# Two-scale attention with a gated convolution on one core: another model in the scheduler, another order of the first transfers, weights converted with more work on ScalarE

## The chip, the cores and the metric

The kernel runs on one core of a Trainium2 chip. The metric is the device time of one execution in microseconds (us). Before the change it is 425.0 us, the median of three runs (424.87 to 425.13).

The engines are named as the profile names them: PE (TensorE, with PEld for its weight loads), DVE (VectorE), ACT (ScalarE), POOL (GpSimd) and SP (SyncE, which here only issues transfers). Each engine executes its own list of instructions in the order in which it was written. An instruction whose input is not there holds up everything behind it on that engine.

## The reference, cut to what matters

```python
q_d, k_d, v_d = mean over 4 neighbouring positions          # B, H, S, D = 8, 8, 576, 64
out_up  = repeat(softmax(q_d @ k_d.T / 8) @ v_d, 4)          # coarse attention, 144 x 144
scores  = where(|i - j| < 4, q @ k.T / 8, -1e9)              # local attention, a band
x       = out_up + softmax(scores) @ v                       # to (8, 576, 512)
gate    = sigmoid(sum over 5 taps of conv_w[t] * x shifted)  # causal, for each channel
out     = (gate * (x @ w_val)) @ w_out                       # w_val, w_out: 512 x 512
```

q, k and v are 32-bit floats. w_val, w_out and conv_w are handed to the kernel as 64-bit floats, and their bits are turned into 32-bit values on the chip.

## The kernel before, in words

**Pairs and blocks.** The attention is cut into 32 pairs p: batch p // 4 and two of its eight heads, whose 2 x 64 channels fill 128 partitions. For the projections x is one long row of 8 x 576 = 4608 columns, cut into eight blocks j of 504 columns and two of 288. Block 0 can be projected when the four pairs of batch 0 are done.

**One pair**, by the names in the profile. Local attention: `sl` (scores on PE), `mx` and `sub` (DVE), the exponential (ACT), `sm` (row sums, DVE, with a small add behind it at L533), `rs` (reciprocal), `pexp` (the two halves of the normalised band, on DVE or POOL), `tl` (two transposes on PE, named tl0 and tl1), `pt` (their copy to SBUF, ACT), `x` (the product with v, PE). Coarse attention: `half` and `qs` (sums of four positions of q and k), `sd` (scores), `cmx` and `cbi` (DVE), `pd` (exponential on ACT; its normalising on DVE, POOL or ACT), `tc` (two transposes), `pdt` (their copy, ACT), `odp` (the product with the coarse v, PE), `od` (its copy, ACT). `xt` on DVE adds the two results. Then `xhs` (rounded part, ACT) and `xls` (remainder) feed the projection; five `gp` steps (the first on ACT, four on DVE) and a tanh on ACT make the gate.

**Products.** A projection is done as three products, high by high, low by high and high by low. A piece of `val` (block j, output chunk c) is three matmuls of 504 columns; `h` = gate * val, which is split into `hh` (ACT) and `hl` (DVE or POOL) and goes through three matmuls for `out`, whose copy `ob` is written to memory.

**Coarse sums.** For batch 0 the sums of four are made on the chip: `half`/`qs` for q and k, `vhalf` (L475) and `vd` (L479) for v, from the loaded `qk` and `vg`. From batch 1 on the transfers make them: one transfer from SP writes the first of four positions, and three more from POOL (L405) add the others to it in memory-to-SBUF accumulation.

**Weights.** w_val and w_out come in 16 chunks of 128 x 256 64-bit numbers (`raw_v`, `raw_o`, L860). For each, ACT takes out two fields (L824 `cv_l`, L826 `cv_a`), DVE makes three passes (L829 shift, L834 sign, L840 add of the low bits), ACT casts to `wh` (L872), and DVE or POOL makes the remainder `wl` (L875). Two raw buffers are there.

**What sets the order.** A list scheduler in the kernel file (`Planner`) is given each operation's engine, a duration in ns, what it depends on and which buffers it needs free. It simulates the engines once, at build time, and the program is written out in that order; where `either` gives two engines, the simulation also picks. Before the change TensorE's order is a fixed list (`tensor_order`, from the strings below); only the other four engines are ordered by due times, some of which are set or shifted by hand in `BIAS`, `FIRST`, `LATE` and `DUE`. A P in the strings is a piece of a projection, a quote mark is the pair before.

```python
START = "sl tl0' tl1' sd tc1' tc0' odp' x'"
START3 = "tl1' sd sl tl0' tc0' tc1' x' odp'"
START4 = "sl tc0' tl1' P tl0' sd tc1' odp' x' P P P"
STEADY = "P P sl tc1' tc0' sd tl1' tl0' P P P P P P odp' x'"
```

Warm-up matmuls (L378, on a constant) are put where the simulation sees TensorE idle.

Of the kernel before, what the change touches and what calls it, by code (L numbers as in the profile page):

```python
# [12 lines left out]
U16 = mybir.dt.uint16  # L13
I64 = mybir.dt.int64
# [5 lines left out]
NC = 4  # L20
P = 128
# [51 lines left out]
def last_reader(b):  # L73
# [7 lines left out]
SB, TB, VB = 3, 2, 3  # L81

# [19 lines left out]
BIAS = {  # L102
    "pdt1": -8000, "h2.0": 2000, "hlo3.0": -1000, "norm1": 2000, "fld": 4000, "h2.1": -8000, "h3.0": -4000,
    "cwfld": 2000, "xl": -8000, "pvb": 2000, "od": -1000, "xt0": -2000, "exp": 1000, "rcp": -2000,
    "cexp0": -1000, "h1.1": 4000, "cmx0": -1000, "hhi3.0": -2000,
}
FIRST = {("qk", 0): -2e6, ("qk2", 0): -1.9e6}
DUE = {("raw", 0): -799008, ("vw", 0): -799729, ("raw", 2): 10251, ("qk", 1): -799570}
# [5 lines left out]

class Planner:
# [25 lines left out]

    def tensor_order(self, order, bufs):
        ops = self.ops
        prev, users = None, {t: [] for t in bufs}
# [12 lines left out]
    def lat(self, o):
        return o["late"] or (self.LOAD if "SP" in o["opts"] else self.LAT)

    def switch(self, a, b):  # L160
# [4 lines left out]
        pairs = {("x", "odp"), ("odp", "x"), ("x", "x"), ("x", "tl"), ("odp", "tl"), ("x", "tc"), ("odp", "tc")}
        return 40 if (a, b) == ("sl", "sd") else 33 if (a, b) in pairs else 3

    def rank(self):
        ops = self.ops
        for o in ops.values():  # L170
            o["in"] = [k for k in o["deps"] + o["free"] if k in ops]
            o["succ"] = []
        for k, o in ops.items():
# [17 lines left out]
        for k, due in ((k, due) for k, due in {**DUE, **FIRST}.items() if k in ops):  # L191
            ops[k]["due"] = due

    def simulate(self):
# [5 lines left out]
        free, queue, events, start, end, who = {}, {}, [], {}, {}, {}  # L200
        for o in ops.values():
            for e in o["opts"]:
                free[e] = self.BEGIN.get(e, 0)
                queue.setdefault(e, [])
        for e, t in free.items():
            events.append((t, e, ()))
        heapq.heapify(events)

        def ready(k):
            for e in ops[k]["opts"]:  # L210
# [915 lines left out]
```

## Time and the profile before

| | |
|---|---|
| median of the runs | 425.0 us |
| span of the profiled execution | 420.9 us |
| PE busy | 382.3 us, 91% |
| DVE busy | 332.8 us, 79% |
| ACT busy | 248.1 us, 59% |
| POOL busy | 122.4 us, 29% |
| moved by DMA | 70.28 MB, mean 167 GB/s |

The execution that was profiled has a span of 420.9 us, from its first to its last instruction; the median of the runs is 4.1 us longer, which is what lies around the span. The busy shares are means over the whole span, and the head of the kernel (loading, converting weights, the first pairs) differs from the steady part.

### The profile page before, as it was taken

The numbers are of one execution on the slowest core, as the hardware profiler recorded it, in microseconds if no ns is written. First come the engines' busy times: TensorE is split into PE (matmuls) and PEld (weight loads), VectorE is DVE, ScalarE is ACT, GpSimd is POOL, SyncE is SP. The second block draws the span as 40 slices with busy tenths as digits, with TensorE's granted clock in tenths as the row PEclk, the third lists the DMA queues.
The fourth block names the chain that finished last, engine by engine and source line by source line (L and its number), as shares of the span: only waits on it lengthen the run. The fifth ranks groups of instructions, "written<-read, shape, count | busy, mean of one in ns | idle before, by whom it ended". The sixth has DMA issues, their size and how long they took to land.

```text
span 420.9 us, 13961 instructions
## 1 busy us (share of the span) xinstructions
PE 382.3 (91%) x5889; PEld 299.6 (71%) x5889; DVE 332.8 (79%) x727; ACT 248.1 (59%) x667; POOL 122.4 (29%) x138
## 2 busy tenths in 40 slices
PE   7757554996999999999999999999999999999996
PEld 4545333775777677777777777777777787778996
DVE  3967667899989997997898789987997877765630
ACT  2646445666777667657667766667657555544321
POOL 4632533175602211531223131311430132040000
PEclk9896765997999999999999999999999999999999
DMA  8979996645697678947797799578964211101102
GB/s 237 303 199 245 306 227 158 142 153 173 191 249 139 167 227 218 217 128 204 205 232 187 213 245 209 138 196 214 208 171 143 85 29 51 55 2 51 49 30 84
DMA packets 25146, 70.28 MB, mean 167 GB/s; under 512 B 3196, under 2 KB 9084, under 8 KB 25084
## 3 DMA queue, kind: packets, MB, share of 16 engines
q1 hardware_dynamic: 19756, 50.65, 37.0%
q0 software_dynamic: 5040, 18.58, 25.4%
q8 instruction: 46, 0.75, 0.8%
q10 hardware_dynamic: 288, 0.16, 0.1%
q14 instruction: 16, 0.13, 0.1%
HBM read 59.94 MB, written 9.44 MB: 165 GB/s over the span
## 4 chain that ended last, share of the span: by engine, by line
PE 64%; DVE 16%; DMA 11%; ACT 4%; issue 3%; SPq 1%; POOL 1%; ACTq 0%; POOLq 0%
PE val L898 7%; PE out L898 7%; PE out L899 7%; PE out L900 7%; PE val L900 7%; PE val L899 7%; DMA vg<-in_vg 5%; PE x L700 4%; PE sd L576 4%; PE tl L650 4%; DVE gp L783 4%; PE odp L736 4%; PE sl L505 4%; DMA raw_v<-in_w_val 3%; PE tc L673 3%
## 5 line engine op out<-in xcount | busy, mean ns | idle before, releaser
L783 DVE SCALAR_TENSOR_TENSOR gp<-xt,cw,gp 128x576 f32<-128x576 f32 x128 | 110.0, 860 | 0.7
L898 PE MATMUL val<-xhs,wh_v 128*128 128x504 f32 (+1 forms) x160 | 63.8, 399 | 0.0
L900 PE MATMUL val<-xls,wh_v 128*128 128x504 f32 (+1 forms) x160 | 60.4, 378 | 0.0
L899 PE MATMUL val<-xhs,wl_v 128*128 128x504 f32 (+1 forms) x160 | 60.3, 377 | 0.0
L898 PE MATMUL out<-hh,wh_o 128*128 128x504 f32 (+1 forms) x144 | 58.2, 404 | 0.0
L899 PE MATMUL out<-hh,wl_o 128*128 128x504 f32 (+1 forms) x144 | 55.5, 385 | 0.0
L900 PE MATMUL out<-hl,wh_o 128*128 128x504 f32 (+1 forms) x144 | 55.3, 384 | 0.0
L711 DVE TENSOR_TENSOR xt<-x,od 128x290 f32<-128x290 f32 x64 | 27.0, 453 | 21.6 <-PE x L700 14.8
L405 POOL DMA_DIRECT2D qs<-in_qkr x21 | 20.3, 967 | 71.9 <-DMA qs<-in_qkr 26.8
L650 PE MATMUL tl<-ident,pexp 128*128 128x128 f32 x160 | 27.1, 301 | 13.5 <-DVE pexp L543 8.2
L543 POOL TENSOR_TENSOR pexp<-sub,rs 64x350 f32<-64x350 f32 x25 | 23.4, 936 | 52.4 <-DVE rs L537 23.4
L576 PE MATMUL sd<-qs 64*64 64x144 f32 x384 | 32.7, 306 | 5.6 <-DMA qs<-in_qkr 4.9
L598 ACT ACTIVATE pd<-sd,cbi 112x144 f32<-112x144 f32 x96 | 35.5, 379 | 3.9 <-DVE cbi L591 3.9
L764 ACT CAST xhs<-xt 128x576 fp32r<-128x576 f32 (+4 forms) x40 | 22.3, 576 | 25.6 <-DVE xt L711 25.3
L655 ACT COPY pt<-tl 128x256 f32<-128x256 f32 (+1 forms) x64 | 26.0, 424 | 18.0 <-PE tl L650 17.9
L948 POOL TENSOR_TENSOR hl<-h,hh 128x504 fp32r<-128x504 f32 (+1 forms) x20 | 25.0, 1250 | 38.6 <-ACT hh L942 31.3
L988 ACT ACTIVATE ob<-out 128x504 f32<-128x504 f32 (+2 forms) x40 | 22.0, 552 | 24.1 <-PE out L900 19.4
L898 PEld LDWEIGHTS val<-xhs,wh_v 128*128 128x128 f32 x160 | 30.6, 191 | 5.6 <-issue 0.6
L900 PEld LDWEIGHTS val<-xls,wh_v 128*128 128x128 f32 x160 | 30.6, 191 | 5.5 <-DVE xls L768 0.2
L650 PEld LDWEIGHTS tl<-ident,pexp 128*128 128x128 f32 x160 | 18.7, 150 | 21.2 <-DVE pexp L543 8.8
L405 POOL DMA_DIRECT2D vs<-in_vgr x21 | 19.6, 933 | 48.7 <-DMA vs<-in_vgr 36.4
L899 PEld LDWEIGHTS val<-xhs,wl_v 128*128 128x128 f32 x160 | 30.7, 192 | 4.0
(96 smaller groups left out, 803.9 us busy)
## 6 DMA issues: line engine op xcount, KB each, us to landing
qk<-in_qk SPq DMA_DIRECT2D x31, 586.0 KB, 6.3
qs<-in_qkr POOLq DMA_DIRECT2D x21, 576.0 KB, 8.0
vw<-in_vw SPq DMA_DIRECT2D x32, 320.0 KB, 6.1
out_t<-ob SPq DMA_DIRECT2D x32, 252.0 KB, 2.5
vs<-in_vgr POOLq DMA_DIRECT2D x21, 288.0 KB, 6.5
qs<-in_qkr SPq DMA_DIRECT2D x7, 576.0 KB
raw_v<-in_w_val SPq DMA_DIRECT2D x8, 256.0 KB, 8.7
raw_o<-in_w_out SPq DMA_DIRECT2D x8, 256.0 KB, 3.3
```

What stands on the lines that cost most here:

```text
L405: nc.gpsimd.dma_start(out=u[nm], in_=src[b, r], accum_op=ALU.add)
L543: eng.tensor_tensor(out=px[r, :, BQ * e : BQ * e + KW], in0=s["ex"][r], in1=s["rs"][r].broadcast_to([64, NSB, KW]), op=ALU.mult,)
L576: nc.tensor.matmul(out=sc[r, i], lhsT=q[r, 48 * i : 48 * i + 64], rhs=s["qd"][r, 1], start=True, stop=True,)
L598: nc.scalar.activation(out=s["pd"][:, g], in_=s["sd"][:, g], func=AF.Exp, scale=1.0 / 128.0, bias=s["bi"][:, g : g + 1], accum_out=s["csm" ...
L650: nc.tensor.transpose(out=tp[:, j], in_=s["px"][:, m : m + 2].rearrange("p a b -> p (a b)"), identity=ident)
L655: nc.scalar.copy(out=s["pt"][:, lo : lo + n], in_=s["tl", u])
L711: nc.vector.tensor_tensor(out=s["xt"][:, 4:].rearrange("p (m a j r) -> p a m j r", m=NPR, a=2, r=2)[:, par], in0=s["x", par].rearrange("p ...
L783: nc.vector.scalar_tensor_tensor(out=s["gp"], in0=s["xt"][:, k : k + S], scalar=cw[:, c, k : k + 1], in1=s["gp"], op0=ALU.mult, op1=ALU.add,)
L898: nc.tensor.matmul(out=o, lhsT=wh[:, d, col], rhs=his[d], start=d == 0, stop=False)
L899: nc.tensor.matmul(out=o, lhsT=wl[:, d, col], rhs=his[d], start=False, stop=False)
L900: nc.tensor.matmul(out=o, lhsT=wh[:, d, col], rhs=los[d], start=False, stop=d == NC - 1)
L948: eng.tensor_tensor(out=t["hl"][:, cs], in0=t["h"][:, cs], in1=t["hh"][:, cs].bitcast(F32), op=ALU.subtract)
```

## The change: what it does

1. **A transfer model.** A class `Transfers` gives the SP queue and the POOL queue a rate each, alone and shared, and the scheduler lets a transfer's data be there when that model says so. The first transfers have a written order (`EARLY`); the tables `BIAS`, `FIRST`, `LATE` and `CNA` are gone.
2. **The port.** Operations with two SBUF inputs are marked; the simulation starts none of these on DVE while POOL is in one, and the other way round, and keeps such work off POOL unless DVE has other work to do.
3. **TensorE's order.** Among the next 14 entries of the list the simulation takes the first that is ready; each kind of operation keeps its order.
4. **Batch 0's v sums** are not made: `odp` of pairs 0 to 3 multiplies with the raw `vg` in 16 matmuls instead of 4. `vg` and `vs` have 80 rows instead of 72 and three buffers instead of two.
5. **Batch 1's q and k sums** are made on the chip (`half`, `qs`) instead of by one SP transfer and three accumulating POOL transfers.
6. **Weights** come in 8 chunks of 128 x 512, with four raw buffers. ACT makes three passes over a chunk (low bits, sign bits, the rest), DVE one (`a`), ACT the cast, DVE or POOL the remainder.
7. The add at L533 is gone: the exponential's tile has an extra column that holds 1e-9.

```diff
-LATE = {"qs": 9000, "vs": 7000}
-CNA = 215
+VROWS = 80
+EARLY = (
+    "qk0 qk2.0 vw0 qk1 raw0 vg0 cwf0 vw1 qk2 raw1 vg1 vw2 qk3 raw2 vg2 vw3 vg3 raw3 "
+    "qk4 vs0.1 vw4 qk5 raw4 vw5 raw5 qk6 raw6 vw6 raw7 qk7 vw7"
+)
+HORIZON = 25000
+SUMB = 2
...
+VSB, RAWB = 3, 4
...
+class Transfers:
...
+    ALONE = {"SP": 0.30, "POOL": 0.16}
+    SHARED = {"SP": 0.15, "POOL": 0.128}
+    FIRST = {"SP": 1500, "POOL": 1950}
+    LANDING = 1600
...
+                if e in ops[k]["port"]:
+                    other = "POOL" if e == "DVE" else "DVE"
+                    if port[other] > now:
+                        heapq.heappush(wake, port[other])
+                        continue
...
-        if p >= NC * FIRSTB:
+        if p >= NC * SUMB:
             return
...
+            if p < NC * FIRSTB:
+                g = s["vg"][0 : SD // 2].rearrange("p a h (r d) -> p a h r d", r=FAC)
+                parts = [(kb, [g[:, kb, h, r] for h in range(2)]) for kb in range(2) for r in range(FAC)]
+            else:
+                parts = [(kb, [s["vd"][:, 2 * kb + h] for h in range(2)]) for kb in range(2)]
+            for i, (kb, w) in enumerate(parts):
                 for h, r in enumerate((LO, HI)):
                     nc.tensor.matmul(
                         out=od_ps[r].rearrange("p (i j) -> p i j", j=GR),
-                        lhsT=s["vd"][:, 2 * kb + h],
+                        lhsT=w[h],
...
+        def fields():
+            nc.scalar.activation(out=low, in_=lo, func=AF.Copy, scale=LOW)
+            nc.scalar.activation(out=top, in_=hi, func=AF.Prelu, scale=2.0**-40, alpha=2.0**100)
+            nc.scalar.activation(out=at.bitcast(F32), in_=hi, func=AF.Copy, scale=2.0**-112)
+
+        def value():
+            nc.vector.scalar_tensor_tensor(
+                out=at, in0=at, scalar=3, in1=bits, op0=ALU.logical_shift_left, op1=ALU.bitwise_or
+            )
...
-        def shift():
-            nc.vector.tensor_scalar(
-                out=t["a"], in0=t["a"], scalar1=3, scalar2=None, op0=ALU.logical_shift_left
-            )
-
-        def sign():
-            nc.vector.scalar_tensor_tensor(
-                out=t["a"], in0=hi, scalar=0x80000000, in1=t["a"], op0=ALU.bitwise_and, op1=ALU.bitwise_or
-            )
...
+        op(("raw", q), "SP", 620, dma, free=[("fld", q - RAWB)], size=P * 512 * 8)
+        op(("fld", q), "ACT", 1700, fields, [("raw", q)], free=[("wlo", q - 2), ("val", q - 1)])
+        op(("val", q), "DVE", 600, value, [("fld", q)], port=ALONE)
+        op(("whi", q), "ACT", 530, hi, [("val", q)])
+        op(("wlo", q), either(600, 1230), 0, lo, [("whi", q)], port=BOTH)
```

What this does to the instructions is shown at three places. The first is the SP queue from its fourth transfer on; numbers behind the names are pair, chunk or batch, and a number behind an underscore only counts buffers. Before:

```order
L427 DMA qk1_173<-in_qk 128x1172
L860 DMA raw_v0_186<-in_w_val 128x256
L432 DMA vg0_201<-in_vg 72x1024
L427 DMA qk2_251<-in_qk 128x1172
L400 DMA qs1_274<-in_qkr 128x1152
L432 DMA vg1_313<-in_vg 72x1024
L436 DMA vw1_322<-in_vw 128x640
L427 DMA qk3_341<-in_qk 128x1172
L436 DMA vw2_393<-in_vw 128x640
L427 DMA qk4_400<-in_qk 128x1172
L432 DMA vg2_464<-in_vg 72x1024
```

The same stretch of the SP queue now:

```order
L584 DMA qk1_125<-in_qk 128x1172
L984 DMA raw_v0_127<-in_w_val 128x512
L589 DMA vg0_129<-in_vg 80x1024
L1136 DMA cw_raw_91<-in_conv_w 128x20
L593 DMA vw1_132<-in_vw 128x640
L584 DMA qk2_188<-in_qk 128x1172
L984 DMA raw_v1_190<-in_w_val 128x512
L589 DMA vg1_196<-in_vg 80x1024
L593 DMA vw2_200<-in_vw 128x640
L584 DMA qk3_206<-in_qk 128x1172
L984 DMA raw_v2_222<-in_w_val 128x512
L589 DMA vg2_226<-in_vg 80x1024
```

qs1 is gone, and the weights' chunks stand between the pairs' inputs from the start: of w_val three quarters are issued by vg2, where one sixteenth of both weights was.

The second place is TensorE around the end of pair 3, which ends the head. Before:

```order
L378 MATMUL sd4_911<-const-bfloat16-1.0 128x350
L576 MATMUL sd4_911<-qs1_274 64x144 x6
L673 MATMUL tc3_1_932<-ident_77,pd3_688 72x112 x3
L378 LDWEIGHTS const-bfloat16-1.0
L378 MATMUL odp3_944<-const-bfloat16-1.0 128x144
...
L378 MATMUL odp3_944<-const-bfloat16-1.0 128x144
L736 MATMUL odp3_944<-pdt3_814,vd3_560 64x144 x4
L700 MATMUL x0_3_960<-pt3_826,vw3_497 64x58 x2
```

The same place now, in two pieces, first from sl5 to the first rows of x of pair 3:

```order
L643 LDWEIGHTS ident_b_78
L643 MATMUL sl5_889<-mask_b_90,ident_b_78 128x350
L650 MATMUL sl5_889<-qk5_490 29x35 x40
L814 MATMUL tc3_1_940<-ident_77,pd3_745 72x112 x3
L791 MATMUL tl4_0_946<-ident_77,pexp0_79 128x128 x3
L841 MATMUL x0_3_955<-pt3_868,vw3_399 64x58 x2
L841 MATMUL x1_3_956<-pt3_868,vw3_399 64x58 x2
```

And behind x of pair 3:

```order
L841 MATMUL x1_3_956<-pt3_868,vw3_399 64x58 x2
L533 LDWEIGHTS const-bfloat16-1.0
L533 MATMUL odp3_987<-const-bfloat16-1.0 128x144
...
L533 MATMUL odp3_987<-const-bfloat16-1.0 128x144
L882 MATMUL odp3_987<-pdt3_842,vg3_420 64x144 x16
```

Before, pair 3 ended with odp and then x, with sd4 (which needs the qs1 transfers) ahead of both. Now sl5 and tl of pair 4 stand ahead of x of pair 3, odp comes last with 16 matmuls, and sd4 (further up) reads sums made on the chip.

The third place is ACT around the copies pdt3 that odp of pair 3 waits for. Before:

```order
L824 ACTIVATE cv_l_892<-raw_v6_873 128x256
L826 ACTIVATE cv_a_894<-raw_v6_873 128x256
L794 ACTIVATE gp1_584<-gp1_584 128x576
L824 ACTIVATE cv_l_900<-raw_v7_885 128x256
L826 ACTIVATE cv_a_902<-raw_v7_885 128x256
L872 CAST wh_v_91<-cv_a_894 128x256
L680 COPY pdt3_814<-tc3_1_932 72x336
L824 ACTIVATE cv_l_940<-raw_o0_908 128x256
```

Now:

```order
L739 ACTIVATE pd4_933,csm4_934<-sd4_853,cbi4_884 112x144 x3
L996 CAST wh_v_95<-a_v3_678 128x512
L821 COPY pdt3_842<-tc3_1_940 72x336
L796 COPY pt4_945<-tl4_0_946 128x384
L762 ACTIVATE pd4_933<-pd4_933,crs4_978 112x144 x3
L965 ACTIVATE bits_o0_1015<-raw_o0_326 128x512
L966 ACTIVATE bits_o0_1015<-raw_o0_326 128x512
L967 ACTIVATE a_o0_1014<-raw_o0_326 128x512
L892 COPY od1_87<-odp3_987 128x288
```

Before, the fields of the last two chunks of w_val stood ahead of pdt3; now all chunks of w_val are behind ACT there, and the next chunk's fields (of w_out) stand behind pdt3, ahead of the copy of odp3.

## Rows read from the trace of the kernel before

**Rows 1.** Busy time by stretch: us, PE, PEld, DVE, ACT, POOL, granted clock, DMA share, GB/s.

```profile
0.00:71.01 71.01, 42.09 (x769) 29.09 (x769) 47.69 (x114) 32.27 (x95) 30.52 (x48) 0.79 0.92 243
71.01:120.07 49.06, 45.75 (x705) 35.22 (x701) 47.59 (x100) 34.29 (x99) 22.86 (x21) 0.88 0.61 166
120.07:331.00 210.93, 207.97 (x3530) 161.59 (x3524) 186.26 (x417) 143.22 (x386) 56.34 (x59) 1.00 0.76 193
0.00:120.07 120.07, 87.84 (x1470) 64.31 (x1470) 95.28 (x213) 66.56 (x192) 53.37 (x69) 0.83 0.79 212
120.07:420.90 300.83, 294.42 (x4426) 235.27 (x4419) 237.50 (x515) 181.58 (x476) 69.03 (x69) 1.00 0.57 149
```

**Rows 2.** What PE waited for, 0 to 71.01 us: total, times, longest.

```profile
PE tl L650 <- DVE pexp L543: 8.2, 2, 5.5
PE odp L736 <- ACT pdt L680: 5.7, 1, 5.7
PE sd L576 <- DMA qs<-in_qkr: 4.9, 1, 4.9
PE tc L673 <- POOL pd L623: 4.3, 1, 4.3
```

**Rows 3.** DVE's groups, 0 to 120.07 us: busy, mean ns, idle before, releaser.

```profile
L783 DVE SCALAR_TENSOR_TENSOR gp<-xt,cw,gp 128x576 f32<-128x576 f32 x28 | 24.9, 894 | 0.1
L543 DVE TENSOR_TENSOR pexp<-sub,rs 64x350 f32<-64x350 f32 x10 | 9.1, 907 | 0.1
L840 DVE TENSOR_TENSOR cv_a<-cv_a,cv_l 128x256 uint16<-128x256 uint16 x16 | 7.9, 495 | 0.0
L829 DVE TENSOR_SCALAR cv_a<-cv_a 128x256 uint32<-128x256 uint32 x16 | 6.3, 391 | 9.5 <-ACT cv_a L826 9.4
...
L834 DVE SCALAR_TENSOR_TENSOR cv_a<-raw_o,cv_a 128x256 uint32<-128x256 uint32 x8 | 4.8, 598 | 0.1
...
L834 DVE SCALAR_TENSOR_TENSOR cv_a<-raw_v,cv_a 128x256 uint32<-128x256 uint32 x8 | 4.0, 499 | 0.0
L467 DVE TENSOR_TENSOR qs<-half 128x144 f32<-128x144 f32 x6 | 3.2, 550 | 0.8 <-POOL half L465 0.8
...
L533 DVE TENSOR_SCALAR sm<-sm 128x10 f32<-128x10 f32 x9 | 1.5, 163 | 0.0
L475 DVE TENSOR_TENSOR vhalf<-vg 72x512 f32<-72x512 f32 x2 | 1.4, 686 | 3.9 <-DMA vg<-in_vg 3.9
L465 DVE TENSOR_TENSOR half<-qk 128x288 f32<-128x288 f32 x3 | 1.3, 441 | 5.5 <-DMA qk<-in_qk 5.5
```

**Rows 4.** ACT's timeline before 69 us: start, duration, what, idle before it.

```profile
66.82 0.43 ACT L824 ACTIVATE cv_l<-raw_v 128x256 uint16<-128x256 uint32 x1 [3.24 <-DMA raw_v<-in_w_val]
67.15 0.41 ACT L826 ACTIVATE cv_a<-raw_v 128x256 f32<-128x256 f32 x1
...
68.59 0.43 ACT L680 COPY pdt<-tc 72x336 f32<-72x336 f32 x1
```

**Rows 5.** PE's timeline at odp of two steady pairs, and x of the second.

```profile
161.61 0.59 PE L736 MATMUL odp<-pdt,vs 72*64 72x144 f32 x6
...
171.95 0.71 PE L736 MATMUL odp<-pdt,vs 72*64 72x144 f32 x8
172.59 0.81 PE L700 MATMUL x<-pt,vw 64*64 64x58 f32 x40
```

**Rows 6.** DVE's and POOL's timelines around 176 us, in order of engine.

```profile
175.84 0.82 DVE L783 SCALAR_TENSOR_TENSOR gp<-xt,cw,gp 128x576 f32<-128x576 f32 x1
...
177.01 1.38 DVE L783 SCALAR_TENSOR_TENSOR gp<-xt,cw,gp 128x576 f32<-128x576 f32 x1
...
176.39 1.38 POOL L948 TENSOR_TENSOR hl<-h,hh 128x504 fp32r<-128x504 f32 x1 [1.75 <-ACT hh L942]
```

**Rows 7.** DVE's groups, 120.07 to 420.9 us.

```profile
L543 DVE TENSOR_TENSOR pexp<-sub,rs 64x350 f32<-64x350 f32 x30 | 20.3, 676 | 0.4
...
L948 DVE TENSOR_TENSOR hl<-h,hh 128x504 fp32r<-128x504 f32 (+2 forms) x22 | 13.3, 610 | 3.4 <-ACT hh L942 3.4
```

More of the change, by code (lines that the diff above doesn't have):

```diff
@@ L13 @@
 U16 = mybir.dt.uint16
+I16 = mybir.dt.int16
 I64 = mybir.dt.int64
@@ L99 @@
 HOLD = 4
[L102 to L108, printed above, removed]
+DUE = {}
+BOTH, ALONE = ("DVE", "POOL"), ("DVE",)
 def either(dve, pool, act=None):
@@ L124, in __init__ @@
+class Planner:
+    RESULT = {"sl": 215, "sd": 220, "tc": 210, "tl": 200, "odp": 245, "x": 300}
+    PIECE = 230
+    SAME = {"DVE": 116, "ACT": 90, "POOL": 150, "PE": 0}
+    CROSS = {
+        "DVE": {"ACT": 116, "PE": 137, "POOL": 250},
+        "ACT": {"DVE": 133, "PE": 153, "POOL": 177},
+        "POOL": {"DVE": 40, "ACT": 40, "PE": 60},
+    }
+    ISSUE = {"SP": 620}
+    BEGIN = {"SP": 700, "ACT": 2450, "PE": 600, "POOL": 3000}
+    WINDOW = 14
+    SHARE = 0.5
     def __init__(self, engines):
@@ L199, in simulate @@
         need = {k: len(o["in"]) for k, o in ops.items()}
[L200 to L210, printed above, removed]
-                heapq.heappush(queue[e], (ops[k]["due"], k))
+        at = {k: {} for k in ops}
@@ new lines, in simulate, with finish @@
+        engines = sorted({e for o in ops.values() for e in o["opts"]}, key="PE ACT DVE POOL SP".split().index)
+        free = {e: self.BEGIN.get(e, 0) for e in engines}
+        ready = {e: [] for e in engines}
+        start, end, who = {}, {}, {}
+        users = {t: [] for t in self.bufs}
+        dma = Transfers()
+        port = {"DVE": 0, "POOL": 0}
+        busy = {"DVE": None}
+        wake = list(free.values())
+        heapq.heapify(wake)
+        head, prev = 0, None
+        def finish(k, t, e):
+            for x in ops[k]["succ"]:
+                need[x] -= 1
+                for to in ops[x]["opts"]:
+                    at[x][to] = max(at[x].get(to, 0), t + self.lat(k, e, to))
+                if need[x] == 0:
+                    release(x)
@@ L241, in simulate, with banks_free @@
-        assert len(start) == len(ops)
+                release(k)
+        def banks_free(k, now):
+            new = {}
+            for tag, _ in ops[k]["banks"]:
+                u = users[tag]
+                i = len(u) + new.get(tag, 0) - self.bufs[tag]
+                new[tag] = new.get(tag, 0) + 1
+                if i >= 0:
+                    for r in u[i]:
+                        if r not in end:
+                            return None
+                        now = max(now, end[r] + self.lat(r, who[r], "PE"))
+            return now
@@ new lines, in pick_tensor @@
+        def pick_tensor(now):
+            streams = set()
+            for i in range(head, min(head + self.WINDOW, len(self.order))):
+                k = self.order[i]
+                if k in start:
+                    continue
+                s = "P" if "." in k[0] else k[0].rstrip("0123456789")
+                if s in streams:
+                    continue
+                if need[k] == 0 and at[k].get("PE", 0) <= now:
+                    t = banks_free(k, now)
+                    if t is not None and t <= now:
+                        return k
+                    if t is not None:
+                        heapq.heappush(wake, t)
+                streams.add(s)
+            return None
```

448 lines of the change are left out of this document (243 added, 205 removed).

## The prediction

> **What bounds the kernel now.** I first cut the span where TensorE's list allows it: at the end of x of pair 3 (71.01 us), of x of pair 7 (120.07 us), and at the last steady pair. The stretches [rows 1] show two different kernels. From 120.07 us on PE is busy for 294.42 of 300.83 us at a granted clock of 1.00: the last 24 pairs and all projections but the first are bound by TensorE, with 6.4 us to win at most. Ahead of that PE is busy for 87.84 of 120.07 us at a granted clock of 0.83, so 32.2 us are idle, and nearly all of that (28.9 us) lies in the first 71.01 us. These are the two parts that I cost: a head of 120 us for 8 pairs, and a body that costs the same whatever happens ahead of it, because odp and x of pair 7 and all that follows on PE stand in the same order before and after (two warm-up matmuls more near the end, and one piece that moved by a place).
>
> What PE waits for in the first 71 us are single long stops [rows 2]: 8.2 us for pexp from DVE, 5.7 us for pdt from ACT, 4.9 us for the qs transfer, 4.3 us for pd from POOL. They look unrelated, but each is an engine that itself stood still behind something that waits for a transfer. ACT's timeline shows one whole [rows 4]: the field of a chunk of w_val waited 3.24 us for its data, and pdt of pair 3 stood behind that at 68.59 us. DVE's idle time tells the same [rows 3]: of 24.8 us (120.07 less 95.28 busy, [rows 1]) 9.5 stand ahead of L829 (ACT's fields, late with the chunks), 3.9 ahead of L475 (vg is late) and 5.5 ahead of the very first half (the first qk). The DMA engines are busy for 0.92 of the first stretch, at 243 GB/s. In the second stretch, 71.01 to 120.07 us, DVE is busy for 47.59 of 49.06 us and PE for 45.75: there DVE is the limit, with PE close behind.
>
> So the head lasts as long as DVE's work in it (95.3 us) plus the time in which DVE waits for transfers or for engines held up by them (24.8 us). I cost the change as a new value for each.
>
> **DVE's work in the head.** From the order of instructions I counted what DVE does up to xt of pair 7, before and now, and priced it by [rows 3]. It loses 16 of L829 (6.3 us), 16 of L840 (7.9), 16 of L834 (4.8 and 4.0), 9 of the add at L533 (1.5), 2 vhalf (1.4), 5 remainders wl of 256 columns, priced as L840, the other two-input pass of that width, at 0.495 (2.5), and 3 gp at 0.894 that now lie behind that point (2.7): 67 instructions, 31.1 us. It gains 8 of the merged pass of 512 columns and 6 remainders of 512 columns. Neither is in the trace; the nearest is gp with 576 columns at 0.894 us, which gives 512/576 of that, 0.79 each, 11.1 us for the 14. (Twice the 256-column pass, 1.0 to 1.2, would be the upper bound, 0.60 for the pass at half the width the lower.) It also gains 8 half at 0.441 (3.5), 3 qs at 0.550 (1.7), 2 pexp at 0.907 (1.8), and 2 xls and 2 hl, which I put at 0.79 too (3.2): 31 instructions, 21.3 us. The net is 36 instructions and 9.8 us less. The durations overlap a little (gp of 0.82 us at 175.84 [rows 6] is followed by the next instruction after 0.74), so 36 of them take back 36 x 0.07 = 2.5 us: 95.3 - 9.8 + 2.5 = 88.0 us.
>
> That is an upper end, because these durations contain the contention with POOL. In [rows 6] POOL's hl began at 176.39 and took 1.38 us; the gp that DVE started beside it took 1.38 instead of 0.82, 0.56 more. In the head POOL has 39 arithmetic instructions before and 21 now. If each of the 18 cost DVE those 0.56 us, 10 us more go: 78 us. The removed rows took their part of it with them (L834 at 0.598 on raw_o, 0.499 on raw_v), so I take less than half of it: **83 us**.
>
> A rule of the Trainium skill speaks against so small a price per instruction: the page "SBUF — State Buffer", section "Who interferes with whom", says that a DVE instruction with two SBUF inputs contends with a GpSimd instruction that reads SBUF, and that the loser of the shared port is blocked for the whole instruction rather than slowed. The sum can do without it; what it would make of the time is among the rivals.
>
> **DVE's waits in the head.** The 9.5 us ahead of L829 were late chunks. The chunks now stand early on the SP queue (three of w_val's four by vg2, in the order shown) and ACT needs three passes for each. [rows 4] price such a pass over 256 columns at 0.33 us, start to start; over 512 columns at most 0.66, so 8 x 3 x 0.66 = 15.8 us, against 16 x 2 x 0.33 = 10.6 before. ACT was busy for 32.27 of 71.01 us [rows 1], so the 5.2 us more fit in. The 3.9 us ahead of vhalf go with vhalf. The 5.5 us ahead of the first qk stay: it is still the first transfer. So 24.8 - 9.5 - 3.9 = 11.4 us. To that I add 1.5 us for transfers that come late in the new order. Bounds: nothing; and what the order implies if all goes at 243 GB/s. Up to qk5, which sl5 ahead of x of pair 3 needs, SP issues 9.7 MB (by the shapes of the order), 40 us, and the three vs1 additions from POOL 1.0 MB, 4 us: there at 44 us. Without any late transfer x of pair 3 would be near 48 us and sl5 some 4 to 6 us ahead of it, so up to 2 us there and as much at two other places: 5.5 us.
>
> Sum for the head: 83 + 11.4 + 1.5 = 95.9 us instead of 120.1, so **-24.2 us**.
>
> **TensorE's side of it.** odp of pairs 0 to 3 has 16 matmuls instead of 4. In [rows 5] four take 0.64 us (171.95 to 172.59), so 12 more are 1.9 us and four pairs 7.7 us. They lie in the first stretch, where PE idles for 28.9 us, and odp of pair 3 now stands behind x of pair 3, so xt waits for it. PE's work in the head becomes 87.8 + 7.7 = 95.5 us at the old granted clock. That is no less than DVE's 95.9 with its waits. What makes room is the clock: 0.79 with PE idle for two fifths, 0.88 in the second stretch, 1.00 in the body [rows 1]; at 0.88 the same work is about 90 us. If the cover is gone, this is the rival below.
>
> **The body.** pexp and hl move from POOL to DVE. Over the whole run DVE has 58 pexp instead of 39 and 35 hl instead of 24; about 17 and 9 of those lie in the body, at 0.676 and 0.610 [rows 7], so 17.0 us, less 23 adds at 0.163 (3.7) [rows 3]: 13.3 us over 24 pairs, 0.55 a pair. DVE's busy share in the steady part is 186.26 of 210.93 us [rows 1]; at one pair in 10.34 us (odp to odp, 161.61 to 171.95 [rows 5]) that is 9.1 us a pair, so 9.7 after. It is under the 10.34 that PE needs, and fewer POOL instructions make it less. I cost the body at nothing, plus 0.3 us for the two warm-up matmuls. PE's work covers it; without the cover every 0.1 us a pair is 2.4 us.
>
> **Sum.** 425.0 - 24.2 + 0.3 = **401 us**. The terms are differences within the profiled execution (span 420.9 us); I put them against the median, 4.1 us above it, whose surplus lies around the span and doesn't change. With the lower value for DVE and no late transfer: 78 + 9.9 = 87.9, 393. With the upper ones: 88.0 + 11.4 + 5.5 = 104.9, 410.
>
> **Rivals.**
> 1. *The head gets faster than that.* If the short chains of waits among engines (the 11.4 us hold about 6 that are not the first load) overlap with what else is ready, now that PE picks among ready pieces, the head is 78 + 6, some 84 us: 389. For it: DVE idles for only 1.5 us in the second stretch. Against: PE would have to do 95.5 us of work at the old clock in 84 us.
> 2. *TensorE bounds the head.* If its clock stays at 0.83, 95.5 us of work, 5.5 us for the first qk and some 3 us of chains are 104 us: 409. For it: the added 7.7 us, and warm-ups that don't hold 1.00 today. Late transfers at the full 5.5 us give the same time.
> 3. *The port blocks in full.* Each of 21 POOL instructions, at about 1 us, stops DVE for its whole length: 21 us, where 83 us contains about 21 x 0.56 = 12. The head is 9 to 11 us longer: 411. It is the page's rule named above. [rows 6] speak against the full price (0.56 of 1.38 us, though the two overlapped only in part), and the simulation avoids such pairs by its own times.
> 4. *It doesn't do what it says.* The modelled landings are wrong, in-order queues again stand behind late data, and only DVE's lighter work is won: 95.3 - 83 = 12 us, less the 3 us of new chains: 416.
> 5. *Slower.* DVE becomes the limit of the body. It decides from 10.34 us a pair, 0.6 above my 9.7; to eat the whole gain it needs 24.2 / 24 = 1.0 above 10.34, 11.3 us a pair, so 1.6 us a pair that no row shows. The pexp rows would have to cost the 0.907 of the head and every other instruction 10% more. At that point 426, more beyond.
>
> **How the numbers follow.** The forecast (392 to 408) has 0.66, rival 1 has 0.10, rival 2 0.12, rival 3 0.04, rival 4 0.04, rival 5 0.04. 401 us is the likeliest. The range of 389 to 411 leaves out rivals 4 and 5, half of 1 and part of 2 and 3. A measurement of this kernel can tell about 0.2%, 0.9 us, from no change: faster 0.95, the same 0.01, slower 0.04.
>
> **What would show it.** Right: x of pair 3 ends near 48 to 53 us and x of pair 7 near 96; DVE's idle time ahead of the weight pass is under 2 us; no stop of PE over 3 us behind the first load; the granted clock of the head is 0.87 or more; the distance from x of pair 7 to the end of the span stays at 300.8 us within 2. Each step has its own sign of failing: ACT's field passes waiting for raw data for more than 3 us (transfer order), PE's busy time over 92 us in the head (odp, clock), gp beside POOL at 1.4 us and more (port), h or xt waits on DVE that PE shows after 120 us (body). Most of all the prediction would be wrong if the head's two engines don't overlap: then neither bound is met and the head is longer than both.

## The result, and the profile after

The changed kernel takes 397.2 us, the median of five runs (395.25 to 397.54), against 425.0 us: 0.934 of the time, 95% interval 0.9305 to 0.9375. That is 27.8 us less; 401 was forecast, with a range of 389 to 411. The span of the profiled execution went from 420.9 to 393.5 us; for the change this is the execution of 395.25 us, the fastest of its five. The ratios further down leave out runs that took over 1.5% longer than the fastest of their kernel, which concerns two of the four of s_pe (412.7 and 412.9 us) and one of e_rows72 (406.9 us).

The page after has PE at 96% of a shorter span. Two of its lines are the engines' shares and, in 40 slices of 9.8 us, the granted clock in tenths, which is at 8 or more in the whole head (it was down to 5):

```profile
PE 378.5 (96%) x5978; PEld 297.4 (76%) x5978; DVE 318.5 (81%) x692; ACT 255.7 (65%) x676; POOL 73.0 (19%) x90
...
PEclk9989899999999999999999999999999999999999
```

The stretches, cut at the same places of TensorE's list (x of pair 3, x of pair 7), answer to [rows 1], with the same columns:

```profile
0.00:50.03 50.03, 41.84 (x908) 30.52 (x909) 35.99 (x90) 32.69 (x90) 12.57 (x30) 0.93 0.97 290
50.03:92.89 42.86, 41.22 (x656) 31.26 (x650) 42.39 (x86) 37.71 (x98) 20.51 (x19) 1.00 0.85 210
92.89:303.60 210.71, 209.03 (x3531) 162.11 (x3526) 188.31 (x416) 145.97 (x396) 36.56 (x39) 1.00 0.76 195
0.00:92.89 92.89, 83.07 (x1558) 61.78 (x1558) 78.38 (x175) 70.41 (x187) 33.08 (x49) 0.96 0.91 253
92.89:393.50 300.61, 295.44 (x4427) 235.59 (x4421) 240.13 (x518) 185.25 (x489) 39.89 (x41) 1.00 0.57 151
```

x of pair 3 now ends at 50.0 us (71.0 before) and x of pair 7 at 92.9 us (120.1): the head is **27.2 us** shorter. The body is 300.61 us, where it was 300.83. So the whole gain lies in the head, 21.0 us of it in its first stretch and 6.2 in the second. DVE is busy for 78.38 us in the head (95.28 before), PE for 83.07 (87.84), at a granted clock of 0.96 instead of 0.83. In the second stretch DVE is busy for 42.39 of 42.86 us.

What PE waits for in the whole head answers to [rows 2]; the four long stops of before are gone, and the largest that are left are stops that wait for nothing that the profile shows:

```profile
PE sl L650 <- issue: 3.9, 3, 2.3
PE odp L882 <- issue: 2.4, 1, 2.4
PE sl L650 <- DMA qk<-in_qk: 0.8, 1, 0.8
```

DVE's groups in the head answer to [rows 3] (busy, mean ns, idle before, releaser):

```profile
L929 DVE SCALAR_TENSOR_TENSOR gp<-xt,cw,gp 128x576 f32<-128x576 f32 x24 | 19.9, 835 | 0.0
L685 DVE TENSOR_TENSOR pexp<-ex,rs 64x350 f32<-64x350 f32 x13 | 6.7, 513 | 0.2
L852 DVE TENSOR_TENSOR xt<-x,od 128x290 f32<-128x290 f32 x14 | 5.9, 447 | 2.4 <-ACT od L892 2.2
...
L623 DVE TENSOR_TENSOR half<-qk 128x288 f32<-128x288 f32 x11 | 5.0, 451 | 5.0 <-DMA qk<-in_qk 5.0
...
L970 DVE SCALAR_TENSOR_TENSOR a_o<-a_o,bits_o 128x512 uint32<-128x512 uint32 x4 | 3.1, 770 | 0.0
L970 DVE SCALAR_TENSOR_TENSOR a_v<-a_v,bits_v 128x512 uint32<-128x512 uint32 x4 | 2.7, 686 | 0.2 <-ACT a_v L967 0.2
L625 DVE TENSOR_TENSOR qs<-half 128x144 f32<-128x144 f32 x9 | 2.7, 303 | 0.7 <-POOL half L623 0.6
...
L999 DVE TENSOR_TENSOR wl_v<-a_v,wh_v 128x512 fp32r<-128x512 f32 x3 | 2.2, 733 | 0.4 <-ACT wh_v L996 0.4
```

pexp is at 0.513 us, where it was 0.907; qs is at 0.303 (0.550); gp is at 0.835 (0.894). The merged weight pass (L970) and the remainder of 512 columns (L999) took 0.68 (wl_o, not shown) to 0.77 us. Of the 24.8 us for which DVE stood still in the head 14.5 are left, 5.0 of them for the first load.

ACT's three passes over a chunk of w_val take 0.78, 0.76 and 0.66 us; in front of them only 1.0 us is lost to late data, for all four chunks together:

```profile
L965 ACT ACTIVATE bits_v<-raw_v 128x512 uint16<-128x512 uint32 x4 | 3.1, 784 | 1.0 <-DMA raw_v<-in_w_val 1.0
...
L966 ACT ACTIVATE bits_v<-raw_v 128x512 int16<-128x512 f32 x4 | 3.1, 763 | 0.0
...
L967 ACT ACTIVATE a_v<-raw_v 128x512 f32<-128x512 f32 x4 | 2.6, 655 | 0.0
```

In the body pexp on DVE went from 30 to 45, and its mean fell (0.676 in [rows 7]):

```profile
L929 DVE SCALAR_TENSOR_TENSOR gp<-xt,cw,gp 128x576 f32<-128x576 f32 x105 | 87.0, 830 | 1.3 <-ACT gp L923 1.1
L685 DVE TENSOR_TENSOR pexp<-ex,rs 64x350 f32<-64x350 f32 x45 | 26.0, 577 | 0.7
```

### The profile page after: what moved, and what is told of

Its sections match the earlier page's. It is cut to its first block, busy times and chain, and to the rows that moved or that the text cites. A ratio compares the mean times of both kernels' runs of the same rounds, so it can differ in the third digit from the quotient of the medians.

```text
span 393.5 us, 13966 instructions
## 1 busy us (share of the span) xinstructions
PE 378.5 (96%) x5978; PEld 297.4 (76%) x5978; DVE 318.5 (81%) x692; ACT 255.7 (65%) x676; POOL 73.0 (19%) x90
## 4 chain that ended last, share of the span: by engine, by line
PE 71%; DVE 13%; DMA 6%; ACT 6%; issue 3%; SPq 1%; ACTq 0%
PE out L1018 7%; PE val L1018 7%; PE out L1019 7%; PE out L1020 7%; PE val L1020 6%; PE val L1019 6%; PE odp L882 5%; PE sd L717 5%; PE sl L650 5%; PE x L841 4%; PE tl L791 4%; DVE gp L929 4%; PE tc L814 4%; DMA out_t<-ob 2%; DMA raw_v<-in_w_val 2%
## 5 line engine op out<-in xcount | busy, mean ns | idle before, releaser
L929 DVE SCALAR_TENSOR_TENSOR gp<-xt,cw,gp 128x576 f32<-128x576 f32 x128 | 106.0, 831 | 1.3 <-ACT gp L923 1.1
L1019 PE MATMUL val<-xhs,wl_v 128*128 128x504 f32 (+1 forms) x160 | 59.3, 371 | 0.0
L1018 PE MATMUL out<-hhl,wh_o 128*128 128x504 f32 (+1 forms) x144 | 58.0, 403 | 0.0
L1019 PE MATMUL out<-hhl,wl_o 128*128 128x504 f32 (+1 forms) x144 | 54.9, 381 | 0.0
L1020 PE MATMUL out<-hhl,wh_o 128*128 128x504 f32 (+1 forms) x144 | 54.9, 381 | 0.0
L1060 ACT CAST hhl<-h 128x504 fp32r<-128x504 f32 (+2 forms) x44 | 22.2, 521 | 22.5 <-DVE h L1046 20.5
L650 PEld LDWEIGHTS sl<-qk 64*29 64x29 f32 x2560 | 25.5, 104 | 11.4 <-issue 9.3
L650 PE MATMUL sl<-qk 64*29 64x35 f32 x2560 | 29.5, 196 | 4.7 <-issue 3.9
L685 DVE TENSOR_TENSOR pexp<-ex,rs 64x350 f32<-64x350 f32 x58 | 32.6, 563 | 0.9
L821 ACT COPY pdt<-tc 72x336 f32<-72x336 f32 x64 | 24.8, 432 | 13.0 <-PE tc L814 12.8
L1018 PEld LDWEIGHTS out<-hhl,wh_o 128*128 128x128 f32 x144 | 27.1, 188 | 5.4 <-issue 0.4
```

Of the source, the lines that this page charges most:

```text
L650: nc.tensor.matmul(out=sc[32 * qd : 32 * qd + BQ, i * KW : (i + 1) * KW], lhsT=t[r, 0, 3 + blk : 3 + blk + BQ], rhs=t[r, 1, blk : blk + KW ...
L685: eng.tensor_tensor(out=px[r, :, BQ * e : BQ * e + KW], in0=s["ex"][r], in1=s["rs"][r].broadcast_to([64, NSB, KW]), op=ALU.mult,)
L821: nc.scalar.copy(out=s["pdt"][:, kb], in_=s["tc", kb])
L929: nc.vector.scalar_tensor_tensor(out=s["gp"], in0=s["xt"][:, k : k + S], scalar=cw[:, c, k : k + 1], in1=s["gp"], op0=ALU.mult, op1=ALU.add,)
L1018: nc.tensor.matmul(out=o, lhsT=wh[:, d, col], rhs=his[d], start=d == 0, stop=False)
L1019: nc.tensor.matmul(out=o, lhsT=wl[:, d, col], rhs=his[d], start=False, stop=False)
```

## The experiments

Three theories were set against each other. **A**, the forecast's: the head is as long as DVE's work in it and DVE's waits. **B**: the transfers set the first stretch, in which the DMA engines are busy for 0.97 of the time. **C**: TensorE sets the head. That the head is DVE's busy time plus its idle time is true of any engine by itself; what a run can test is whether more work on DVE makes the head longer. Runs whose name begins with e undo one part of the change, and the scheduler then makes a new plan of the whole head; runs that begin with s keep every instruction at its place and add or take one cost. All ratios are against the kernel before on the same chip, and the change itself stands at 0.934. "Head" is the end of x of pair 7 in the profiled execution, 92.9 us for the change; its first stretch ends with x of pair 3 (50.0 us).

**e_vsum**: batch 0's v sums on the chip, 4 matmuls per odp.

```diff
-                parts = [(kb, [g[:, kb, h, r] for h in range(2)]) for kb in range(2) for r in range(FAC)]
+                parts = [(kb, [g[:, kb, h, 0] for h in range(2)]) for kb in range(2)]
...
+            op(("pva", p), either(602, 1225), 0, pool_v(0), [("vg", p)], free=[("pvb", p - 2)], port=BOTH)
+            op(("pvb", p), either(335, 690), 0, pool_v(1), [("pva", p)], port=BOTH)
```

> The v sums of batch 0 are made on the chip again (two additions a pair, on DVE or POOL), and odp of pairs 0 to 3 has 4 matmuls again; all else as after the change, planned anew. Theory A (the head is as long as DVE's work in it and its waits): DVE gets 6 of the 8 additions, at 0.69 and about 0.4 us some 3 us, and each odp waits for vg and two additions instead of vg alone: 399 to 403 us against 397. Theory B (transfers set the first stretch): the same bytes, 397 within 1. Theory C (TensorE sets the head): 7.7 us less work for PE, 390 to 394.

Measured: 0.9589 (0.9534 to 0.9644), about 10 us more than the change. The head is 102.5 us with DVE busy for 85.3 us in it. The sign speaks against C: with 12 matmuls fewer in each of four odp the head is 9.6 us longer. (TensorE is busy for 83.07 us in it, as in the change, at a lower granted clock of 0.92, so the saving of 7.7 us doesn't show.) The size is above A's 2 to 6 us; the four first and two second additions that went to DVE (2.7 and 0.8 us) are half of DVE's 7 us more, the rest comes with another plan.

**e_sumb1**: batch 1's q and k sums by transfers.

```diff
-SUMB = 2
+SUMB = 1
```

> Batch 1's q and k sums come by four transfers of 590 KB again instead of 16 additions on the chip; planned anew. Theory A: DVE loses 9 of the additions, about 3.5 us: 394 to 397 us, unless the added bytes hold something up. Theory B: 2.36 MB more in a stretch in which the DMA engines are busy for 0.97 at 289 GB/s, 8 us: 403 to 406. Theory C: 397.

Measured: 0.9642 (0.9605 to 0.9679), about 13 us more; the head ends at 106.0 us. Of that 7.6 us are two stops at pair 4 in PE's timeline, and the granted clock of the second stretch is 0.91 instead of 1.00:

```profile
59.66 2.55 PE L717 MATMUL sd<-qs 64*64 64x144 f32 x24 [3.18 <-DMA qs<-in_qkr]
...
69.85 1.33 PE L841 MATMUL x<-pt,vw 64*64 64x58 f32 x36 [4.42 <-ACT pd L739]
```

sd of pair 4 waits 3.18 us for the qs transfer (it was 4.9 us before the change, [rows 2]), at a time that the chain of four transfers sets, and x of the same pair 4.42 us for work that ACT had queued ahead. A had the sign wrong here, though it had named the case (added bytes that hold something up): the additions taken from DVE don't pay for the wait. B's 8 us are nearer, but s_dma below, with added bytes and the same plan, loses nothing.

**e_noport**: the scheduler without the port rule.

```diff
-            port=port,
+            port=(),
```

> The port rule is taken out of the scheduler's simulation; all else as after. POOL then has 92 arithmetic instructions instead of 36, DVE 646 instead of 692. Price by the row of before (0.56 us of DVE for each POOL instruction): DVE loses 46 x 0.55 = 25 us of work and gains 56 x 0.56 = 31 us of contention over the run; in the head about a third, so some 2 to 4 us there, and a body that stays bound by PE: 398 to 402. Rival, the port blocks in full (about 1 us each): 56 us on DVE, 10 to 18 us more in the head, over 406. Rival, no contention worth the name: 394 or less.

Measured: 0.9794 (0.9746 to 0.9843), about 19 us more, outside the 398 to 402. Windows of head and body, and two DVE groups of the body:

```profile
0.00:101.44 101.44, 84.88 (x1566) 63.14 (x1566) 86.78 (x164) 67.14 (x171) 52.37 (x67) 0.95 0.83 225
101.44:411.10 309.66, 295.70 (x4428) 235.55 (x4421) 241.58 (x483) 180.29 (x476) 78.49 (x80) 1.00 0.56 149
```

```profile
L929 DVE SCALAR_TENSOR_TENSOR gp<-xt,cw,gp 128x576 f32<-128x576 f32 x100 | 91.1, 911 | 1.3 <-ACT gp L923 1.1
...
L685 DVE TENSOR_TENSOR pexp<-ex,rs 64x350 f32<-64x350 f32 x23 | 22.8, 992 | 0.7
```

The head is 8.6 us longer with DVE busy for 8.4 us more, though DVE has fewer instructions. The body is 9.1 us longer, which nothing in the forecast allowed for: pexp there is at 0.992 instead of 0.577, gp at 0.911 instead of 0.830. Those two cost 9.5 + 8.1 = 17.6 us of DVE for 38 more arithmetic instructions of POOL in the body (51 against 13; the 80 and 41 of the rows hold the issues of transfers too), 0.46 us each on the mean. The run is over the 406 that I set as the mark of a port that blocks in full; half of the loss came in the body, which that expectation had left out. (What a single collision costs is read under rival 3 below.) DVE isn't full in the body (241.58 of 309.66 us), yet TensorE loses time there: tl waits for pdt in 9 places, 8.2 us, where it was 1.4 us in 2. What makes pdt late was not followed further, and POOL is also slower at the work itself (1.04 us for a pexp), so the 19 us are the worth of the rule in the plan and not of the contention alone.

**e_noearly**: no written order for the first transfers (`EARLY = ""`).

> The written order of the first transfers is empty; the scheduler's due times order them, with the transfer model kept. If the order of the first transfers is what took the waits away: 402 to 412 us, with DVE idle ahead of what the late transfers bring. If the transfer model alone does it: 397 within 2.

Measured: 0.9337 (0.9290 to 0.9383), no different from the change.

```profile
0.00:91.74 91.74, 81.63 (x1569) 61.85 (x1569) 80.33 (x174) 69.95 (x187) 32.24 (x51) 0.98 0.95 258
91.74:390.60 298.86, 295.21 (x4426) 235.71 (x4421) 239.55 (x520) 185.87 (x491) 37.42 (x38) 1.00 0.57 152
```

The transfer model and the due times order the first loads as well as the table does. The written order explains none of the gain.

**s_dve**: DVE's mx three times for pairs 0 to 7.

```diff
-            nc.vector.tensor_reduce(out=s["mx"], in_=s3, axis=AX.X, op=ALU.max)
+            for _ in range(3 if p < 2 * NC else 1):
+                nc.vector.tensor_reduce(out=s["mx"], in_=s3, axis=AX.X, op=ALU.max)
```

> The kernel after the change with every instruction in the same order, but the maximum over the local scores (mx) of pairs 0 to 7 is taken three times instead of once: 16 passes more on DVE at 0.43 us, 6.9 us in the head; the result stays the same. Ratio of the change itself: 0.934. Theory A (DVE and its waits set the head): 3.4 us (the second half of the head alone, where DVE is busy for 41.7 of 42.1 us) to 6.9 us more, a ratio of 0.942 to 0.950. Theory B (transfers) or C (TensorE): 1 us more at most, 0.936.

Measured: 0.9444 (0.9405 to 0.9483), 4.4 us more for 6.9 us of added work: A's range.

```profile
0.00:50.32 50.32, 40.25 (x908) 29.41 (x909) 41.03 (x101) 32.78 (x90) 12.52 (x30) 0.97 0.92 284
50.32:95.69 45.37, 42.01 (x656) 30.99 (x650) 44.93 (x91) 37.53 (x97) 18.65 (x20) 1.00 0.85 204
0.00:95.69 95.69, 82.26 (x1558) 60.40 (x1558) 85.96 (x191) 70.31 (x186) 31.17 (x50) 0.98 0.89 246
```

DVE is busy for 85.96 us in a head of 95.69: part of the added work takes the place of idle time (14.5 to 9.7 us), and the rest shows in the head. The two stretches differ here. In the first, DVE is busy for 5.0 us more (41.03 against 35.99) and the stretch is 0.3 us longer; in the second it is busy for 2.5 us more and the stretch is 2.5 us longer. So by this run A holds for the second stretch, and in the first DVE's work has room to spare: it is not what sets it.

**s_pe**: odp of pairs 0 to 3 done twice.

```diff
-            for i, (kb, w) in enumerate(parts):
+            for i, (kb, w) in [x for _ in range(2 if p < NC * FIRSTB else 1) for x in enumerate(parts)]:
```

> The kernel after the change with every instruction in the same order, but the 16 matmuls of odp of pairs 0 to 3 are done twice, the second time from the start: 8.4 us more of TensorE work in the head. Theory C: 8 us more, 0.953. Theory A or B: TensorE is idle for 9.8 us of 93, so most of it hides; but od, and with it xt, comes 2.1 us later for four pairs: 0 to 4 us more, 0.934 to 0.943.

Measured: 0.9616 (0.9556 to 0.9677), some 12 us more, above all three. The first stretch takes 7.8 us more, in which TensorE is busy for 4.8 us more, and DVE's largest wait in the head shows a way that it takes:

```profile
0.00:57.84 57.84, 46.66 (x1005) 35.98 (x1005) 35.20 (x90) 32.39 (x89) 12.36 (x30) 0.94 0.86 258
```

```profile
DVE xt L852 <- ACT od L892: 10.2, 4, 4.8
```

xt waits 10.2 us for od, the copy of odp, where it waited 2.2 us. By itself the run speaks for C; the next one tries it the other way round.

**s_odp4**: odp of pairs 0 to 3 with 4 matmuls in place of 16, so three of each four v values are left out.

```diff
-                parts = [(kb, [g[:, kb, h, r] for h in range(2)]) for kb in range(2) for r in range(FAC)]
+                parts = [(kb, [g[:, kb, h, r] for h in range(2)]) for kb in range(2) for r in range(1)]
```

> The kernel after the change with every instruction in the same order, but odp of pairs 0 to 3 has 4 matmuls instead of 16: only the first of each four v values is used, the other three are left out. TensorE has 7.7 us less to do, and od comes 1.9 us earlier for four pairs. If the price of the 16 matmuls is hidden as forecast: 0.934 within 0.003. If it is on the path, as the run with twice the odp suggests (11 us for 8.4): 7 to 10 us less, 0.911 to 0.918.

Measured: 0.9387 (0.9322 to 0.9452): nothing gained.

```profile
0.00:49.38 49.38, 37.88 (x837) 26.82 (x837) 35.05 (x90) 32.34 (x89) 12.38 (x30) 0.90 0.97 291
...
0.00:92.43 92.43, 78.30 (x1462) 56.32 (x1462) 77.86 (x175) 70.24 (x187) 32.81 (x49) 0.94 0.91 250
```

PE has 4.8 us less in the head (78.30 against 83.07) and the head is 92.4 us instead of 92.9. The 12 added matmuls of each odp are hidden, and C is wrong in that less work on TensorE gains nothing; 16 more on top of them (s_pe) are not hidden, and xt then waits 8.0 us longer for od.

**s_dma**: vg and vs with 128 rows.

```diff
-VROWS = 80
+VROWS = 128
```

(The sizes that the scheduler reckons with stay those of 80 rows.)

> The kernel after the change in the same order, but vg and vs have 128 rows instead of 80 (48 rows of padding that nothing reads): 0.79 MB more for vg, 0.79 MB for the four transfers of vs1, some for vs2, all in the head. Theory B (the DMA engines set the first stretch, busy for 0.97 of it at 290 GB/s): 1.2 to 1.6 MB more ahead of x of pair 3, 4 to 5 us, 0.943 to 0.946. Theory A or C: 0 to 2 us, 0.934 to 0.939.

Measured: 0.9370 (0.9339 to 0.9401), within A's range. B is wrong:

```profile
0.00:47.96 47.96, 41.11 (x909) 29.72 (x909) 35.24 (x90) 32.39 (x90) 12.66 (x30) 0.96 0.95 333
...
0.00:91.42 91.42, 82.39 (x1558) 60.96 (x1558) 78.45 (x175) 71.10 (x189) 33.03 (x49) 0.98 0.92 281
```

The first stretch is not longer (47.96 us, 50.03 for the change) though the engines moved 333 GB/s in it instead of 290. At a busy share of 0.97 they were not at their limit. More bytes don't lengthen the stretch; whether transfers that come at other times would is not tried by this.

**e_dve3**: the weights' sign and low bits on DVE again (the three passes of before over 512 columns, two on ACT; the raw buffer stays in use until DVE has read it).

```diff
-        op(("fld", q), "ACT", 1700, fields, [("raw", q)], free=[("wlo", q - 2), ("val", q - 1)])
-        op(("val", q), "DVE", 600, value, [("fld", q)], port=ALONE)
+        op(("fld", q), "ACT", 1150, fields, [("raw", q)], free=[("wlo", q - 2), ("val", q - 1)])
+        op(("val", q), "DVE", 1500, value, [("fld", q)], port=ALONE)
```

> The weights' sign and low bits go back to DVE: two passes on ACT and three on DVE for a chunk of 128 x 512, as before the change but in 8 chunks; planned anew. DVE gets 16 passes more, together 8 x 1.2 us by the rows at 256 columns, and ACT 8 fewer of 0.62 to 0.77 us. Theory A: 8 to 10 us more, 0.953 to 0.958. If ACT was what held the head: 4 us less, 0.925. If neither: 0.934.

Measured: 0.9731 (0.9697 to 0.9765), 16.6 us more, the second costliest part to take away.

```profile
0.00:109.65 109.65, 93.28 (x1577) 68.73 (x1577) 89.42 (x188) 65.28 (x175) 39.93 (x56) 0.89 0.81 218
```

DVE is busy for 89.42 us in the head, 11.0 more, near the 8 to 10 of A; the head is 16.8 us longer, so 5.7 us are added waits, which A didn't have.

**v_pool**: an attempt at a faster version: the v sums of pairs 1 to 3 on POOL.

```diff
+        if 0 < p < NC * FIRSTB:
+            op(("pva", p), {"POOL": 1225}, 0, pool_v(0), [("vg", p)], free=[("pvb", p - 2)], port=BOTH)
+            op(("pvb", p), {"POOL": 690}, 0, pool_v(1), [("pva", p)], port=BOTH)
```

> As after, but the v sums of pairs 1 to 3 are made on POOL (two additions a pair, 1.3 and 0.8 us, written over the first quarter of vg) and their odp has 4 matmuls; pair 0 keeps 16; planned anew. If the 16 matmuls are on the path and POOL's additions, started when vg lands, come in time: 3 to 6 us less than the change, 0.920 to 0.927. If DVE beside them pays 0.56 us for each of six additions and the rest is hidden: 0.936 to 0.942. The scheduler makes another plan for the whole head, which by the runs so far can move it by several us either way.

Measured: 0.9417 (0.9367 to 0.9467), 3 us slower than the change. It takes away TensorE work that s_odp4 shows to be hidden and adds work on POOL; DVE is busy for 82.2 us in the head, 3.9 more.

**e_w1**: TensorE's order fixed again (`WINDOW = 1` in the scheduler).

> TensorE's order is the fixed list again (a window of one entry), all else as after; planned anew. If the choice among ready pieces is what filled TensorE's waits in the head: the long stops at the head of the list come back, 6 to 12 us more, 0.948 to 0.962. If the transfers and DVE's lighter work did it: 0.934 within 0.004.

Measured: 0.9420 (0.9362 to 0.9479), 3 us more, between the two expectations; the choice among ready pieces is worth little.

**e_rows72**: `VROWS = 72`.

> vg and vs have 72 rows as before instead of 80; planned anew. If 72 rows make these transfers slow (the chain of before held 12.5 us of one vg): 3 to 8 us more, 0.941 to 0.953. If transfers don't set the head, as the run with 128 rows says (0.937): 0.934 within 0.004, apart from what another plan does.

Measured: 0.9456 (0.9374 to 0.9537), about 5 us more, but the interval is too wide, and the plan too different, to say that the rows did it. This stays open.

## Why the prediction was right

**The head and the body.** Right. All of the gain lies ahead of x of pair 7 (27.2 us; 24.2 forecast), and the body cost nothing (-0.2 us; +0.3).

**DVE's work.** The term that was mis-sized: 83 us forecast, 78.4 measured, next to the lower bound of 78. The prices of the new passes were fair (0.79 against 0.68 to 0.77). What failed is the step that took less than half of the contention off. pexp fell by 0.39 us on 13, qs by 0.25 on 9, gp by 0.06 on 24: 5.1 + 2.2 + 1.4 = 8.7 us, of the 10 that 18 fewer POOL instructions at 0.56 could give. e_noport shows the same from the other side: without the port rule DVE's busy time in the head rises by 8.4 us. That this work sets the head is borne out for the second stretch, where DVE is busy for 42.39 of 42.86 us and s_dve's added work shows in full. For the first stretch, with 21.0 of the 27.2 us, it is not: there s_dve hid 5.0 us of added work. What went from that stretch is TensorE's idle time (28.9 us before, 8.2 now), above all the four stops of [rows 2].

**DVE's waits.** 12.9 us forecast, 14.5 measured. That the two add up to only 3.0 us too much is in part luck: 4.6 us too much for the work, 1.6 too little for the waits. The waits for chunks and for vg are gone as reckoned; the part for late transfers (1.5) isn't there, and short waits for sd, sl and od took its place (2.4, 1.8 and 2.2 us). The bound for late transfers rested on 243 GB/s; the first stretch ran at 290, and s_dma at 333.

**TensorE.** The 16 matmuls are hidden, as costed (s_odp4), but with little to spare (s_pe). Their price was too high: taking 12 of 16 away saves 4.8 us of TensorE's busy time, where 7.7 were forecast. The 95.5 us of work at the old clock became 83.1, by that lower price and by the granted clock, which went from 0.83 to 0.96; 0.87 or more was the sign that I named.

**The rivals.** Rival 1 (389) holds half: DVE's work was at its lower bound, but the waits were not. Rival 2 didn't come: its clock of 0.83 was 0.96, and in s_odp4 less work on TensorE gained nothing. Rival 3 needs a closer look, since the rule of the Trainium skill that it rests on holds in the rows. In the head after, POOL's wl_v and the gp beside it:

```profile
36.75 1.27 POOL L999 TENSOR_TENSOR wl_v<-a_v,wh_v 128x512 fp32r<-128x512 f32 x1 [1.27 <-ACT wh_v L996]
```

```profile
37.25 1.40 DVE L929 SCALAR_TENSOR_TENSOR gp<-xt,cw,gp 128x576 f32<-128x576 f32 x1
```

POOL's instruction ended at 38.02 us and gp 0.63 us later. In [rows 6] it is 177.77 and 178.39, 0.62 later. In both the two ran side by side for about 0.77 us, so they alone can't tell a block from a slower gp. A pair of e_noport, side by side for 0.92 us, can:

```profile
205.29 1.48 POOL L914 TENSOR_TENSOR xls<-xt,xhs 128x576 fp32r<-128x576 f32 x1 [1.40 <-ACT xhs L910]
```

```profile
205.85 1.53 DVE L929 SCALAR_TENSOR_TENSOR gp<-xt,cw,gp 128x576 f32<-128x576 f32 x1
```

Here gp takes 1.53 us and again ends 0.61 us after POOL's instruction (207.38 and 206.77): 0.16 us more side by side than in [rows 6] made it 0.15 us longer (1.53 against 1.38), so a gp beside POOL stands still and doesn't just run slower. DVE is blocked until POOL's instruction ends, which is what the Trainium skill says ("SBUF — State Buffer", "Who interferes with whom"); my reading of 0.56 us as a smaller price was wrong, it was the rest of an instruction that had begun earlier, and the sign that I named for this step (gp beside POOL at 1.4 us) did come. What kept rival 3's time away is that 14 of the 21 POOL instructions in the head cost DVE nothing: ten ran beside no DVE instruction with two SBUF inputs, and four more made none of those beside them longer. Rival 4 needs the modelled landings to be wrong; e_noearly, whose order of first loads comes from the model and the due times, is as fast. Rival 5 didn't come (188.31 of 210.71 us busy in the steady part), but e_noport lost 9.1 us in the body with DVE busy for 78% of it.

**What stays open.** Which part of the change shortened the first stretch. In every e run x of pair 3 still ends between 44.9 and 53.2 us (71.0 before), so none of the parts that were undone brings it back, and no run took away the transfer model or the larger chunks with their four buffers. The e runs change a part and the plan with it. By s_dve, which keeps the plan, DVE's work is worth 0.6 us a microsecond over the head, all of it in the second stretch; the costs of single parts (16.6, 13, 10, 19 us) add up to more than 27.8, and each contains some us of the scheduler's luck. That the 1.8 us around the span (395.25 us for 393.5) are less than the 4.1 that I read before has no effect on the sum: 4.1 was a median less another execution's span.

## What to carry to other kernels

When two engines are both near full in a stretch, price the change on each, and then add a known cost to one at a time with the order kept: that told apart what undoing parts could not. Read the answer for each stretch by itself: the same added work was hidden in one and showed in full in the next. A contended row holds its contention: where the partner engine loses its work, take the row's price from a place where it ran alone. And a list scheduler's model of contention can be worth more than any instruction it moves: here planning without the port rule cost 19 us, the most of all parts that were taken away.

## What was not expected of the hardware

TensorE stops in the middle of a group of matmuls that waits for nothing that the profile shows, in the stretch in which the DMA engines are busiest; and the granted clock fell in the stretches of 10 us that hold the ends of the two longest. PE's timeline and three windows of the change:

```profile
20.95 0.45 PE L650 MATMUL sl<-qk 64*29 64x35 f32 x31 [2.31 <-issue]
...
41.11 1.69 PE L882 MATMUL odp<-pdt,vg 72*64 72x144 f32 x22 [2.36 <-issue]
```

```profile
20.00:30.00 10.00, 8.70 (x140) 6.93 (x139) 6.64 (x16) 7.08 (x19) 1.09 (x2) 0.83 0.95 281
30.00:40.00 10.00, 8.15 (x244) 5.93 (x242) 9.71 (x23) 8.57 (x24) 2.66 (x3) 1.00 0.99 325
40.00:50.00 10.00, 8.89 (x176) 6.81 (x176) 6.31 (x16) 6.04 (x17) 4.17 (x5) 0.83 1.05 288
```

The stops last 2.31 and 2.36 us; in the two windows that hold their ends the clock is 0.83 on the mean, so TensorE was at 1.2 GHz for part of them, and at 2.4 GHz throughout between them (1.00). Ahead of each fall it had stood still for those 2.3 us. It doesn't always fall: in s_pe a stop of 2.45 us ends at 28.89 us, and the clock is 1.00 from 20 to 40 us. In the second stop of the change a packet of the instruction queue begins in the quarter of a microsecond from 38.75 us:

```profile
q8 instruction: 1, 0.02, 23.9%
```

Ahead of the first, which begins at 18.63 us, one begins between 18.25 and 18.50 us. But others begin between 25 and 26, 31 and 32 and 44 and 45 us with no long stop beside them, and the row doesn't say for which engine. That TensorE waits there for its own instructions, fetched behind the data, is one reading, and no run here tried it. The longest stops of this kind were 3.9 us (s_odp4) and 4.7 us (v_pool), so some of the scatter between plans may be theirs.
